# Attention then a squared-ReLU MLP on one core: query tiles 1 and 3 of batch 0 moved from an f32 path to an f16 one, with a new instruction order

## The chip, the cores and the metric

The kernel runs on one core of a Trainium2 chip. The metric is the device time of one execution in microseconds (us), of which the median over several executions is compared. The core has a matrix engine (TensorE, PE in the profile, its weight loads PEld), a vector engine (VectorE, DVE), a scalar engine (ScalarE, ACT), a general engine (GpSimd, POOL), and SyncE (SP), whose queue issues every transfer of this kernel, in order. Each engine works through its own queue in order and waits where an operand is not ready.

## What is computed

The reference, cut to what matters (4 batches, 8 heads, 576 positions, head dimension 64; then 2304 rows of 512 through 2048 hidden values):

```python
q_rot, k_rot = (rotate(q), rotate(k))
scores = scale * np.matmul(q_rot, k_rot.transpose(0, 1, 3, 2))
scores = scores - np.max(scores, axis=-1, keepdims=True)
attn = np.exp(scores)
attn = attn / (np.sum(attn, axis=-1, keepdims=True) + 1e-09)
x = np.matmul(attn, v)            # heads joined to rows of 512
h = x @ w_in
r = np.maximum(h, 0.0)
out = (s * (r * r) + b) @ w_out
```

The result has to hold f32 accuracy.

## The kernel before, in words

**Tiles.** Heads are taken in pairs; a batch has four pairs, the kernel sixteen, numbered 0 to 15. A pair has nine query tiles of 128 rows: 0 to 3 and 4 to 7 are its main rows (two tiles for each head in each half), 8 holds the last 64 rows of both heads. Half a batch's rows form a *unit* of the MLP: tiles 0 to 3 of batch 0 are unit 0, tiles 4 to 7 of batch 0 are unit 1, and so on up to unit 7; unit 8 is all the tiles 8.

**One query tile** (`attend`, line 185) is: scores on PE into PSUM (`s_tile`, lines 590 to 603), their minimum after scaling on DVE (`s_max`, line 609), the exponential and its sum on ACT (`s_exp`, through the helper on line 372), a reciprocal on DVE (line 637). Then the probabilities have to be transposed and multiplied by V, and for that there are two paths.

- **The f16 path** splits every f32 number into two f16 numbers, high and low. `p_a` writes the high part (ACT line 372, DVE line 364 or POOL line 366), `p_b` the low part (DVE line 369), both into the buffer `pab`; `p_t` (line 665) transposes `pab` by a DMA from SP into a `pt` buffer; `pv_sum` (line 687) multiplies with V, in 28 f16 matmuls of 64 weight columns, and ACT (`o_out`) copies the result to `x`. A `pt` buffer has room for two tiles.
- **The f32 path** normalizes in place (`p_norm`), transposes on PE by matmuls with the identity (`p_T`, lines 721 and 723, into the PSUM buffer `po`), copies PSUM to a `pt` buffer (`p_ev`: ACT line 372 or DVE line 711) and multiplies in f32 (`pv32`, line 740).

Which tiles go the f32 path is set by `is_g` on line 116: pairs 0 to 3 (batch 0), tiles below 4 with `i % 2 < GT`. With `GT = 2` those are all of tiles 0 to 3. Both paths' `pt` tiles share two buffers.

**Unit 0** has an MLP of its own in f32 on the unsplit weights (`mlp_in0`, line 833; `mlp_out0`, line 857, with `out_sum0`, which copies `po` to SBUF on ACT). Its two 128-row halves, j = 0 and 1, take the two halves of one `po` buffer. Meanwhile the weights, loaded as f64 bit patterns (`load_w`, line 400) and put together to f32 words (`w_sign`, `w_low`, `w_rebias`, `w_join`, all into the array `wio` through staging buffers `x`), are measured by `w_gram` on PE (line 438) and split into f16 pairs (`w_hi`, `w_lo`, DVE line 369, `wio<-wio,wsc`). Units 1 to 8 run on the f16 pairs: `x_hi` and `x_lo` split the attention output into `xa`, then `mlp_in` (line 807, 12 matmuls for each of 16 blocks f) and `mlp_out` (line 877).

**What sets the order.** `plan()` lists 2690 steps. Three strings fix the rest: `ORDER` is the sequence of the steps (two characters each), `PICKS` the engine of every step that may run on several, `SLOTS` the buffer of every step that takes one. The tables come from a search made ahead of time. In `plan()` several steps that fill different parts of one buffer (the two halves of `po`, for instance) have no edge between them. The framework adds a wait wherever two steps touch one buffer and one of them writes.

```python
GT = 2
def is_g(pr, i):
    return pr < HP and i < 4 and i % 2 < GT
def alone(pr, i):
    return is_g(pr, i) or i == 8 or (GT == 1 and pr < HP and i < 4)
def width(pr, i):
    return 64 if i == 8 else P if GT == 1 and pr < HP and i < 4 else 256
# in attend(), for a tile of the f32 path, and else:
add((ACT, DVE, POOL), "p_norm", *c, r=[("r", (pr, g))], w=[("p", c)])
add(PE, "p_T", *c, r=[("p", c), ("tab",)], w=[("po", c)])
add((ACT, DVE), "p_ev", *c, r=[("po", c)], p=[("pt", pr, "j", t)])
add((ACT, DVE, POOL), "p_a", *c, r=[("p", c), ("r", (pr, g))], p=[("pab", c)])
add(DVE, "p_b", *c, r=[("p", c), ("r", (pr, g))], w=[("pab", c)])
add(DMA, "p_t", *c, r=[("pab", c)], p=[("pt", pr, j // 2)])
```

Of the kernel before, what the change touches and what calls it, by code (L numbers as in the profile page):

```python
# [19 lines left out]
GT = 2  # L20
# [7 lines left out]
B, H, S, D, DM, DFF, P = 4, 8, 576, 64, 512, 2048, 128  # L28
# [9 lines left out]
    "DVAADUDTDoAWDWDXDYDZAQDeDaDlDfDgDbDcDdDpDmDqAZDrAYATASDzARD0AUDsDtD2DnAXD3DhDjAJALAMDiDkADDuD1DvD4DwDxAaAwDyAKAyAFJuAGEC"  # L38
    "AzD5EFJvAbAVJ2EeAEAxD7D6A0AND8JwJxJyENEDEGEQAHEREEAqEHEIEJAcAIAOESJ3EKAjJzAkAdAmAlD_AfAgAeAnEOAPArJ4J5J6ELEPEMEcEdD9EgEh"
    "AtAsEfAoEiAhEqJ0A9A3EVETEWEjEUEkBAA_A4ElA-EZA5J7BBEmAuJ1D-KAKBKIKJEnErBEA6BHAiEoApAvJ8EsA1EzEAFREXEaE2FUEpA2J9KCEvKDEwKE"  # L40
    "J-BFKKKLKFA7EtEuKMBGE5J_EYE0BKEbEBKGKHKNBIA8BME3BRBCKaExKSKOKPBXFBBLFCBUBSKTKbBNBTBVBDBOKUE6KcKVKdK2KQBJBPK3KWE1BYBaBZBb"
# [4 lines left out]
    "McLrMTMRdIMdMUMoMpL9CwE4E7MqMrMzbtbzbyMwC5MeC8MFMSGgFsbubxb0M0MxMyMhb1MfMsC2NOMGM1bvNBbwMiC7C6DGMVNPM2DHM3b2MHDIE8FWb3M7"
    "NCNQE9E-NDDJFXE_FAFHNRMjMgDMM8FYFJC9FZFab4b5CdNmCXM-M4FICeM_MkMlDPNANSNnNTM5FKb9b6b8NpCkCqb_DODNNoGjFNDQNUFqNENFNqCrMtFt"
    "NrFrNsFuNGFLM6FOM9FjFhNJDKNHb-NYNbcAcBcCcJcIb7cHMuNcNZF1NtFkF4NKFiNuNaMvFvFMNINLGEGFFlNxF2F5NvcKNdcLNeNfNycMcUOAcNcTdJcW"
    "NgOBN2N3OCN4NMNNNhF3NiNVFmNjODOEFnOFN5OGdKN6N7cVcXcYFwOOcDcEcFORFxOPFoFyNkNlFzOHF0dLOQdMdNDLC3CxOSC4F7dOdPGIOLOIN8OMFPOT"
# [951 lines left out]
```

## Time and profile before

| what | value |
|---|---|
| median of 3 executions | 642.1 us (642.1, 645.03, 641.84) |
| the profiled execution: its own time | 644.86 us |
| the profiled execution: span, first to last instruction | 643.1 us |
| mean granted TensorE clock, as a share of full speed | 0.970 |
| PE busy | 591.7 us, 92% of the span |
| DVE busy | 478.3 us, 74% |
| ACT busy | 421.8 us, 66% |
| POOL busy | 130.5 us, 20% |
| DMA | 90.67 MB, mean 141 GB/s |

The page of the profile gives each engine's busy time, then the span in 40 slices of 16 us, a digit a slice (9 is 90% or more). PEclk, in the same slices, is the clock that TensorE was granted. Rows of groups, waits and the order of time carry the line of the kernel (L857), the engine, the operation, and the tiles as output<-input. A matmul row's own time is longer than its share of the engine, since matmuls overlap; where it matters, the distance from one start to the next is taken.

### The profile page before, as it was taken

Reading aid. Unit: us, or ns where it says so; the run is one execution under the profiler, and the core shown is the slowest. Engines: PE = TensorE matmul, PEld = TensorE weight load, DVE = VectorE, ACT = ScalarE, POOL = GpSimd, SP = SyncE. Lnnn points to the kernel's source line nnn. Section 1 sums busy time; section 2 is a strip of 40 time slices with the busy share of each in tenths; the row PEclk is TensorE's granted clock in tenths of the full one; section 3 lists DMA queues with packets and bytes.
Section 4 is the critical chain, followed back from the end, with each engine's and each line's share of the span. In section 5 each row is a group of like instructions: output and inputs, shape, how many; then the busy total and the mean of one; then the engine's idle time right before and its main releaser. Section 6 shows DMA issues by size and latency. Waiting matters only on the chain. (4 is left out here: it accounts for less than half of the span.)

```text
span 643.1 us, 13206 instructions
## 1 busy us (share of the span) xinstructions
PE 591.7 (92%) x5054; PEld 398.7 (62%) x5054; DVE 478.3 (74%) x1035; ACT 421.8 (66%) x872; POOL 130.5 (20%) x138
## 2 busy tenths in 40 slices
PE   2356999998979999999989999999999999999996
PEld 2234566677637657667656666667665766766863
DVE  5797989998978999898987898888677355633101
ACT  5686889778878997777667786574673556422411
POOL 0313455211011323121022022102111102110210
PEclk9666999999989999999999999999999999999999
DMA  8899477896937595889546867557465022170100
GB/s 288 248 241 251 159 227 224 211 188 145 184 92 180 120 176 128 193 216 187 112 94 132 168 152 147 130 131 150 107 134 125 20 70 57 32 149 1 34 1 33
DMA packets 207376, 90.67 MB, mean 141 GB/s; under 512 B 189393, under 2 KB 193617, under 8 KB 207313
## 3 DMA queue, kind: packets, MB, share of 16 engines
q1 hardware_dynamic: 207312, 89.83, 59.7%
q8 instruction: 39, 0.64, 0.4%
q14 instruction: 25, 0.20, 0.1%
HBM read 31.97 MB, written 4.72 MB: 57 GB/s over the span
## 5 line engine op out<-in xcount | busy, mean ns | idle before, releaser
L877 PE MATMUL po<-wio,g 128*128 128x512 f16 x768 | 185.2, 379 | 1.0 <-DVE o L369 1.0
L807 PE MATMUL px<-xa,wio 128*128 128x256 f16 x1536 | 183.3, 273 | 0.0
L807 PEld LDWEIGHTS <-wio 128*128 128x128 f16 x1536 | 147.6, 98 | 34.4 <-issue 2.9
L372 ACT ACTIVATE p<-s,nm 128x576 f32<-128x576 f32 x144 | 105.7, 735 | 49.8 <-DVE s L609 35.8
L609 DVE TENSOR_SCALAR_CACHE_REDUCE s<-s,es 128x576 f32<-128x576 f32 x135 | 109.2, 819 | 30.4 <-PE s L603 29.3
L877 PEld LDWEIGHTS <-g 128*128 128x128 f16 x768 | 71.6, 98 | 72.2 <-issue 3.9
L369 DVE SCALAR_TENSOR_TENSOR pab<-p,sum,pab 128x576 f16<-128x576 f32 x128 | 107.0, 846 | 7.9 <-POOL pab L366 3.8
L372 ACT ACTIVATE hr<-px,xc 128x512 f32<-128x512 f32 x64 | 43.7, 683 | 77.5 <-PE px L807 76.3
L825 POOL TENSOR_TENSOR g<-hr,g 128x512 f16<-128x512 f32 x34 | 41.6, 1226 | 225.8 <-DVE g L711 98.7
L372 ACT ACTIVATE pab<-p,sum 128x576 f16<-128x576 f32 x62 | 47.2, 767 | 12.5 <-DVE sum L637 5.6
L366 POOL TENSOR_SCALAR pab<-p,sum 128x576 f16<-128x576 f32 x35 | 31.4, 899 | 118.3 <-DVE sum L637 74.5
L602 PE MATMUL s<-kS,qkT 128*128 128x512 f16 (+1 forms) x150 | 52.6, 386 | 2.1 <-DMA kS<-qkT 2.1
L602 PE MATMUL s<-qkT 128*128 128x512 f16 (+1 forms) x150 | 53.0, 391 | 1.1 <-ACT p L372 1.0
L711 DVE CAST g<-hr 128x512 f16<-128x512 f32 x30 | 12.8, 426 | 54.8 <-ACT hr L372 35.5
L687 PE MATMUL px<-pt,v 128*64 128x256 f16 (+1 forms) x880 | 51.0, 247 | 1.8 <-DMA pt<-pab 1.8
L602 PEld LDWEIGHTS <-qkT 128*128 128x128 f16 (+1 forms) x300 | 28.6, 103 | 32.8 <-issue 8.9
L687 PEld LDWEIGHTS <-v 128*64 128x64 f16 x880 | 36.5, 110 | 14.7 <-issue 12.3
L372 ACT ACTIVATE hr<-hr 128x512 f32<-128x512 f32 x68 | 42.6, 628 | 1.5
L366 POOL TENSOR_SCALAR wio<-x 128x512 bf16<-128x512 f32 (+1 forms) x32 | 28.5, 901 | 58.2 <-ACT x L372 21.1
L833 PEld LDWEIGHTS px<-x,wio 128*128 128x128 f32 x256 | 30.6, 192 | 4.5 <-issue 2.0
L833 PE MATMUL px<-x,wio 128*128 128x128 f32 x256 | 33.0, 280 | 0.1
L603 PEld LDWEIGHTS <-qkT 128*128 128x128 f16 (+1 forms) x300 | 27.8, 101 | 7.6 <-issue 3.2
(137 smaller groups left out, 853.9 us busy)
## 6 DMA issues: line engine op xcount, KB each, us to landing
x<-in_moe_w_in_dram SPq DMA_DIRECT2D x16, 512.0 KB, 5.1
x<-in_moe_w_out_dram SPq DMA_DIRECT2D x16, 512.0 KB, 4.4
st_v<-in_v_dram SPq DMA_DIRECT2D x16, 320.0 KB, 4.0
st_q<-in_q_dram SPq DMA_DIRECT2D x16, 288.0 KB, 3.8
st_k<-in_k_dram SPq DMA_DIRECT2D x16, 288.0 KB, 3.9
kS<-qkT SPq DMA_DIRECT2D x30, 144.0 KB, 2.6
out_dram<-o SPq DMA_DIRECT2D x7, 512.0 KB, 3.4
vS<-v SPq DMA_DIRECT2D x32, 64.0 KB, 2.1
```

The lines of the kernel that those rows point to most:

```text
L366: eng.tensor_scalar(out=out, in0=in0, scalar1=s1, scalar2=s2, op0=op0, op1=op1)
L369: nc.vector.scalar_tensor_tensor(out=out, in0=in0, scalar=scalar, in1=in1, op0=op0, op1=op1)
L372: nc.scalar.activation(out=out, in_=in_, func=func, **kw)
L602: nc.tensor.matmul(ps[rows, MAIN:2 * MAIN], lhs, kk[:, 4 * h:4 * h + 4], start=(n == 0), stop=(n == 1))
L603: nc.tensor.matmul(ps[rows, MAIN - TAIL:MAIN], lhs, kk[:, 8, 64 * h:64 * h + 64], start=(n == 0), stop=(n == 1))
L609: nc.vector.tensor_scalar(out=T["s"], in0=T["s"], scalar1=-1.0 / 8.0 if pr in FQ else st[pr]["es"], scalar2=None, op0=ALU.mult, op1=ALU.mi ...
L687: nc.tensor.matmul(o[64 * h:64 * h + 64, 0:n], v_rows(pr, h, k, z), pv_rhs(pr, i, h, k), start=((z, k) == todo[0]), stop=((z, k) == todo[-1]))
L711: nc.vector.tensor_copy(out, in_)
L807: nc.tensor.matmul(ph, w16[0][:, f, wz, cc], X["xa"][:, xz, c], start=(c == 0 and n == 0), stop=(c == NC - 1 and n == 2))
L825: (nc.vector if eng == DVE else nc.gpsimd).tensor_tensor(out=g[:, 1], in0=r, in1=g[:, 0], op=ALU.subtract)
L833: nc.tensor.matmul(ph, wi[:, f + 1, c * P:(c + 1) * P], xs[0]["x"][:, c, j * P:(j + 1) * P], start=(c == 0), stop=(c == NC - 1))
L877: nc.tensor.matmul(po, g[:, gz, jj], w16[1][:, f, wz], start=(n == 1 and i == 0), stop=(n == NF and i == 2))
```

## The change

`GT` is 1 in place of 2. Of batch 0's query tiles 0 to 3, tiles 1 and 3 (of all four pairs, eight tiles) now go the f16 path, tiles 0 and 2 stay on the f32 path. Unit 0's MLP stays in f32. For the eight tiles `p_norm`, `p_T`, `p_ev` fall away, and `p_a`, `p_b`, `p_t` come in; the four `pv32` of half j = 1 become four `pv_sum` with 128 output columns. All three tables are new: the order of all steps, the picks and the buffers. Nothing else in the file differs (a table is one line shorter, so its lines are numbered one lower).

```diff
-GT = 2
+GT = 1
 ORDER = (
-    "DVAADUDTDoAWDWDXDYDZAQDeDaDlDfDgDbDcDdDpDmDqAZDrAYATASDzARD0AUDsDtD2DnAXD3DhDjAJALAMDiDkADDuD1DvD4DwDxAaAwDyAKAyAFJuAGEC"
...
+    "DTAAEDDUEEECDbDcDdEGDeDhEHEFAQDiEIEQDfDgEREJEKENELAJESEMALATASDjDkJ2DoDqEOEPEVAMEWJ3JuJvAKETADDtAFJ4AEAGAHEUDrDpJ5J6DzAN"
...
 PICKS = (
...
 SLOTS = (
...
```

Four counts from the new order against the old, of what each queue holds ahead of unit 1's first f16 MLP matmul (on PE) and of the `x_lo` or `x_hi` of unit 1 that it needs (DVE, ACT):

| queue | steps before | steps now | what differs |
|---|---|---|---|
| PE | 186 | 175 | `p_T` 16 to 8, `pv32` 8 to 4, `pv_sum` 9 to 12, `mlp_out0` 30 to 28 |
| DVE | 322 | 314 | `p_b` 26 to 32, `p_ev` 4 to 0, `w_lo` 18 to 13, `s_max` 46 to 44, `w_sign` 9 to 12, `w_low` 4 to 6, `p_a` 4 to 2; `p_s` 14 to 10, one `g0`, `p_norm` and `v_hi` less, one `w_hi` more |
| ACT | 240 | 242 | `p_a` 17 to 26, `p_ev` 12 to 8, `p_norm` 11 to 7, `p_s` 18 to 22, `w_hi` 12 to 8, `w_low` 19 to 23, five kinds by one or two |
| SP | transposes among the loads of w_out: 5 before the last load | 8 of tiles 1 and 3 and one more | see the third place below |

**First place: PE, the work on a tile 1 or 3.** Before, in the stretch in which unit 0's tiles are finished (`s` is a score tile, `p` the probabilities, `st_v` V in f32):

```order
L590 MATMUL s_1076<-xa_197,xa_199 128x512
L591 MATMUL s_1076<-xa_197,xa_199 128x64
L721 MATMUL po<-ident,p_1022 128x128 x4
L723 MATMUL po<-ident,p_1022 64x128 x2
L740 MATMUL px_1102<-pt_1008,st_v_270 64x128 x10
L602 LDWEIGHTS qkT_325
```

Now, at the first tile pair of the new path (the two rows of L686 go on in this way to 28 pairs):

```order
L589 MATMUL s_942<-xa_146,xa_181 128x512
L590 MATMUL s_942<-xa_146,xa_181 128x64
L686 LDWEIGHTS v_355
L686 MATMUL px_948<-pt_924,v_355 64x128
L686 LDWEIGHTS v_355
L686 MATMUL px_948<-pt_926,v_355 64x128
```

The transposes are gone from PE, and the product with V reads two `pt` buffers that a DMA fills.

**Second place: ACT, around the copies of unit 0's result** (`o<-po` is `out_sum0`; PE's next `mlp_out0` or `mlp_out` writes `po`). Before, the copy of half 0:

```order
L372 ACTIVATE g_2060<-g_2060,sb 128x512
L372 ACTIVATE wio<-wio,wsc 128x512
L372 ACTIVATE pab_2199<-p_2133,sum_2132 128x576
L372 ACTIVATE o<-po 128x512
L372 ACTIVATE wio<-wio,wsc 128x512
```

and on PE, where this copy falls in between the two rows of `mlp_out0` with x2:

```order
L772 MATMUL px_2149<-g_2130,ones16b 128x256
L857 MATMUL po<-wio,hr_1848 128x512
L382 MATMUL px_2155<-mx,ones_99 128x3
L857 MATMUL po<-wio,hr_1848 128x512 x2
L857 MATMUL po<-wio,g_1951 128x512 x2
L602 LDWEIGHTS qkT_2139
```

Now both copies stand together on ACT:

```order
L371 ACTIVATE pab_2392<-p_2305,sum 128x576
L371 ACTIVATE p_2407,sum_2386<-s_2362,nm_2384 128x576
L371 ACTIVATE o<-po 128x512
L371 ACTIVATE g_2422<-hr_2375 128x512
L371 ACTIVATE o<-po 128x512
```

and PE has all of `mlp_out0` behind it by then; the last rows of it and what follows:

```order
L602 LDWEIGHTS qkT_2175
L602 MATMUL s_2362<-kS_2188,qkT_2175 128x64
L856 MATMUL po<-wio,g_2251 128x512 x4
L381 MATMUL px_2432<-mx,ones_99 128x3
L806 LDWEIGHTS wio
L806 MATMUL px_2434<-xa_2211,wio 128x256
```

The copy of half 0 no longer stands between two matmuls into the same buffer.

**Third place: SP, the loads of w_out** (`x` is a staging buffer of a weight block, `pt<-pab` a transpose). Before:

```order
L400 DMA x_1082<-in_moe_w_out_dram 128x1024
L490 DMA st_v_1164<-in_v_dram 128x640
L400 DMA x_1192<-in_moe_w_out_dram 128x1024
L665 DMA_TRANSPOSE pt_1197<-pab_975 128x9x128
L665 DMA_TRANSPOSE pt_1199<-pab_1115 128x9x128
L490 DMA st_v_1201<-in_v_dram 128x640
```

Now:

```order
L399 DMA x_909<-in_moe_w_out_dram 128x1024
L664 DMA_TRANSPOSE pt_924<-pab_849 128x9x128
L664 DMA_TRANSPOSE pt_926<-pab_671 128x9x128
L399 DMA x_929<-in_moe_w_out_dram 128x1024
L399 DMA x_988<-in_moe_w_out_dram 128x1024
L664 DMA_TRANSPOSE pt_1018<-pab_804 128x9x128
L399 DMA x_1020<-in_moe_w_out_dram 128x1024
```

Eight loads of w_out now stand behind the first of the new transposes, and the last of them (block 12) behind all eight.

## Rows read from the trace of the kernel before

**Rows 1.** The page: busy time of each engine, and TensorE's clock in 40 slices.

```profile
PE 591.7 (92%) x5054; PEld 398.7 (62%) x5054; DVE 478.3 (74%) x1035; ACT 421.8 (66%) x872; POOL 130.5 (20%) x138
...
PEclk9666999999989999999999999999999999999999
```

**Rows 2.** Busy time by stretch (from:to, length, then columns PE, PEld, DVE, ACT, POOL, PEclk, DMA share, GB/s).

```profile
0.00:64.00 64.00, 30.25 (x193) 20.07 (x194) 47.96 (x102) 44.36 (x88) 14.42 (x20) 0.74 0.89 256
64.00:192.00 128.00, 119.26 (x1053) 82.70 (x1052) 116.59 (x274) 108.15 (x232) 38.31 (x45) 0.98 0.73 180
192.00:643.00 451.00, 442.15 (x3811) 295.95 (x3809) 313.76 (x661) 269.33 (x553) 77.75 (x73) 1.00 0.52 114
```

**Rows 3.** PE's waits, 64 to 210 us: total, times, longest.

```profile
PE po L857 <- ACT o L372: 3.6, 1, 3.6
```

**Rows 4.** DVE's waits, 64 to 210 us: total, times, longest.

```profile
DVE s L609 <- PE s L603: 5.9, 5, 3.6
```

**Rows 5.** PE in order of time (start, duration): a `p_T`, what follows it, a `pv32`.

```profile
76.64 0.66 PE L721 MATMUL po<-ident,p 128*128 128x128 f32 x4 [0.21 <-ACT p L372]
...
77.60 0.39 PE L602 MATMUL s<-qkT 128*128 128x512 f16 x1
...
81.22 1.46 PE L740 MATMUL px<-pt,st_v 128*64 128x128 f32 x20 [0.20 <-DVE wmx L441]
```

**Rows 6.** PE in order of time: a `pv_sum` of 64 columns, one of 256, what follows.

```profile
151.89 0.35 PE L687 MATMUL px<-pt,v 128*64 128x64 f16 x10
...
152.45 1.12 PE L857 MATMUL po<-wio,g 128*128 128x512 f32 x2
...
158.14 0.74 PE L687 MATMUL px<-pt,v 128*64 128x256 f16 x10
...
159.79 1.16 PE L833 MATMUL px<-x,wio 128*128 128x128 f32 x8
```

**Rows 7.** PE in order of time: `mlp_out0` ahead of and behind a wait; first f16 `mlp_in`.

```profile
166.52 1.88 PE L857 MATMUL po<-wio,g 128*128 128x512 f32 x4
...
182.76 2.50 PE L857 MATMUL po<-wio,hr 128*128 128x512 f32 x4 [3.62 <-ACT o L372]
185.06 3.10 PE L857 MATMUL po<-wio,g 128*128 128x512 f32 x4
...
193.85 2.78 PE L807 MATMUL px<-xa,wio 128*128 128x256 f16 x24
```

**Rows 8.** PE by stretch of 4 us (columns PE, PEclk, DMA share, GB/s).

```profile
180.00:184.00 4.00, 1.24 (x3) 1.00 0.69 164
184.00:188.00 4.00, 4.00 (x7) 0.57 0.00 0
```

**Rows 9.** ACT in order of time: the copy that PE waited for.

```profile
182.13 0.58 ACT L372 ACTIVATE o<-po 128x512 f32<-128x512 f32 x1
```

**Rows 10.** Groups of instructions by shape on DVE (count, busy us, mean ns).

```profile
L609 DVE TENSOR_SCALAR_CACHE_REDUCE s<-s,es 128x576 f32<-128x576 f32 x135 | 109.2, 819 | 30.4 <-PE s L603 29.3 <-ACT p L372 0.9
L369 DVE SCALAR_TENSOR_TENSOR pab<-p,sum,pab 128x576 f16<-128x576 f32 x128 | 107.0, 846 | 7.9 <-POOL pab L366 3.8 <-ACT pab L372 3.8
...
L369 DVE SCALAR_TENSOR_TENSOR wio<-wio,wsc 128x512 f16<-128x512 f32 x32 | 24.0, 750 | 1.0 <-POOL wio L366 0.5 <-ACT wio L372 0.4
...
L364 DVE TENSOR_SCALAR pab<-p,sum 128x576 f16<-128x576 f32 x31 | 16.5, 538 | 0.5
...
L364 DVE TENSOR_SCALAR wio<-x 128x512 uint16<-128x512 uint16 x13 | 7.3, 560 | 4.9 <-ACT x L372 3.5 <-DMA x<-in_moe_w_in_dram 0.6 <-DMA x<-in_moe_w_out_dram 0.5
...
L711 DVE COPY pt<-po 128x640 f32<-128x640 f32 x4 | 3.3, 821 | 0.0
```

**Rows 11.** The transposes of line 665: duration on SP (ns, min/median/max), then issue to landing.

```profile
L665 SPq DMA_TRANSPOSE pt<-pab x128: 1242/1308/2727, 103.7 to 575.8; - x128
...
DMA to landing us min/median/max: 2.8/2.9/5.6
```

**Rows 12.** DVE in order of time: its first rotation.

```profile
7.06 0.76 DVE L527 TENSOR_TENSOR z<-st_q,tab 128x576 f32<-128x576 f32 x1 [1.52 <-DMA st_q<-in_q_dram]
```

More of the change, by code (lines that the diff above doesn't have):

```diff
@@ new lines @@
+    "KtBaBZBYDnBbBKFQBLLUKeJ_KqK-BxABKrKuBMKvKfBNKYLaKQA1K_BOByLABzB0LbKwLBB1KRLVLWKZBeBJBgFFKxBhBfBPBQA2LcK2KgKhBwLIBWBcKyB2"
+    "BkBnB4B7BiLdLeLJBdK3FsB-FSBmLKK4KzCBLLB6BlB5BoB8BjBpLiL0BqLCFGB_CAB3L1LMLDK5LfCSK6LjCCCTLgLEK0FUCUK1KiKjCVboLNCWL2LkLOFD"
+    "dBCLE4COE7CDB9MICNL3CMClbpL-bmbnCEMJL4CPLlCYFTL5CnMKL_CmCoCpLPLXCZCyFVK7CbbqL6CaEbCcMLMMLmLYLZE8K8FbbrMAbsCsMmdCC1C0CvLn"
+    "CuMBE9MndDLodECtLhCFCGCwdFMCE-CzE_MNMoMpdGFAGGMDFvMqC2MEFedHbtbubvMZb0byLpCfMOCIdIMPFfCHLqLsMaLtLrCiCgChCJCjFHFILuMQLvbw"
@@ new lines @@
+    "CXbzbxCdMWFcCeLwMXC_K9LFb1MTb2FJLGLxMULyLHMYDMDGDOMbMcDBDIb8b-CKCQMwMzMRFgFdCRDAMdDCMxM0L7LzFqMeMfDDb_L8MrMyL9M1DJb9NOFt"
+    "MsNPMFC5NBNQMGNmMHFKC6MhM2DHMiNncTdJb3cAcBNCcVcWcUMVMSGFC8NRNSNoM-CqCkMjMgb4dKDKM3NTNUDPCrM_GIM7cXNDcYC7M4GSM5M8F1MkNpFW"
+    "dLcZMlDNNANENqNrcCb5FXdMFYb6DENYb7C9FZFaNFNZFNNGNsC3CxC-C4DFFLMtNJcacbDQMuDRdNGJFjFkDLNbcccDcENKNHM6M9FOMvFhNcNdNaNLNIFi"
+    "NtFPODdOcFOANuNeNxNfOEDSNgFrGENjFlF2OBNvdnNhF3NkNMNVdPdQOCNyNwNzFMOFFnOGOHNNcKcHcIOON2NWcJGHN3FuNXN4OIOPN5cLOLcMcNcgORce"
@@ new lines @@
+    "NlNiGgFoFwcfcdchOSdROTGPGQGROJOQFxF4N6dSFyFzOUOMOVN7ciOZOsOecGcjOfGTckOgF0OaOtN0OvcsclcqGBOwF5N8OWOuN1dTF6dUOxdVF9docrcp"
+    "cOOhcmOXdpGUdqF-drdWctcuOyFmOKN9GCONGfOiOzF7dXdYN-OjN_O3cvO8O0OkdZdscPGKO9GDO4O-ObOYOlOmdaGLF8FpdbGjOpGMGNGOOnOqdccncoPN"
+    "cwO_PAOcOdeRc3cxeScyddcQGbPBPCGiPKHUGeG6G9F_O5eTdeO1eUGAO2POdfeVeWPDeXPLPEeYeZPPPMPQeadgPRGsebGVGXGYHXPSc0c2czQWc1cRdhc4"
+    "c5PVdiPaPbQXPTdjdkedecOrOoc6PHeeefdlQYenemO6Pdc7PFPIGtGhdmQZeodtepGWGpduQaPePcO7egQbPGG4GZG5PUc8c9c-PfGqdvehdwGaPJGcc_eq"
@@ L89 @@
[L89 to L91 removed]
+    "GSSVVSGSSVSSGVSGVSGSGVSSVSSGSSGSSVSGVVGGSSGVSGSSGSSVSGGGSGGSVSSGSSVSSGVGGSSGSGGSSVGGGSSVSGVSGGSGVVSSSVVSSSVVSSSVVGSSVVSS"
+    "SVVSGSVVSSGGVGGSVVSSSVVGSSVVSGSGVSGVVVSSSVVSSSVGSGGVVGSSSSSSSSSSSSVSVSSSSSSSSVSSSSVSSGVSVSSSSGSSSSSSSSSVSSVGSSSSVSVSSSSS"
@@ L104 @@
+    "210100101102000011020130213110304211113002011110010022340011030110210101101342120131100310111303002101231100041120121311"
+    "132011030101010114030001101120110102130110130211004102011112000001030301101210101101323010010201000410501043010100001021"
+    "100002362201410131001101132100043201000100102114011210301410000103110002001110110041103110100121130021011021010011401111"
+    "00010110120021010010100013301011142032010104001003011043110210004110110200231101000110012101010010020010"
 )
```

99 lines of the change are left out of this document (40 added, 59 removed).

## The prediction

> **What bounds the kernel now.** I read the page first. Over the whole span PE is busy 92% of the time [rows 1], so whatever shortens PE's queue is worth looking at; but an average says nothing of the stage that the change touches. So the next view is busy time by stretch [rows 2], and it shows three stages. In 0 to 64 us PE does 30.25 us of work and the granted clock is 0.74: PE is waiting for loads and for the work on DVE and ACT. In 64 to 192 us, where batch 0 is finished and unit 0 has its f32 MLP, PE is busy 119.26 of 128 us (93%), but DVE is busy 116.59 (91%) and ACT 108.15 (84%). From 192 us on PE has 442.15 us of work in 451 us, and DVE only 313.76. The first f16 MLP matmul, that of unit 1, starts at 193.85 us [rows 7]. It is my milestone: behind it PE alone paces the kernel, so the change gains what it brings that matmul forward, less what work it leaves over for later.
>
> The waits say what the idle time of the middle stage is. The largest single one on PE is 3.62 us, for a copy on ACT [rows 3]: the first `mlp_out0` of half 1 writes the other half of the `po` that `out_sum0` of half 0 reads, and starts at 182.76 [rows 7], right after the copy of 0.58 us that began at 182.13 [rows 9]. What the wait leaves behind is seen in two more rows. PE was busy only 1.24 of the 4 us before 184, and the granted clock of the next 4 us is 0.57 [rows 8], so near the lower of its two levels (1.2 GHz, half of 2.4). The two L857 rows there take 2.50 and 3.10 us, where the same row at full clock took 1.88 [rows 7]. DVE waits for a score tile for up to 3.6 us [rows 4]: PE's queue holds that tile behind the stalled matmul.
>
> **The change part by part.** *PE, work.* A `p_T` took from 76.64 to 77.60, 0.96 us [rows 5]; eight fall away, 7.7 us. A `pv32` took 1.46 [rows 5]; four fall away, 5.8 us. Four `pv_sum` of 128 columns come in. The trace has none of that width, so it is bounded by the two next to it: with 64 columns 151.89 to 152.45, 0.56 us, with 256 columns 158.14 to 159.79, 1.65 us [rows 6]. By the line between them 128 columns take 0.56 + 1.09/3 = 0.92, and four 3.7 us (bounds 2.2 and 6.6). PE's work: -7.7 - 5.8 + 3.7 = **-9.8 us**.
>
> *PE, the stall.* In the new order (second place) both `out_sum0` stand behind all of `mlp_out0`, and between the last `mlp_out0` and the next write to `po` PE has unit 1's first `mlp_in`, each more than 1 us of work (2.78 for the row of two [rows 7]) against two copies of 0.58 us. So the 3.6 us go, and with them the slow clock's extra (2.50 + 3.10 - 2 x 1.88 = 1.84). If the cover were gone, a wait of the same size would be back. If PE alone set the pace, the sum would be -9.8 - 3.6 - 1.8 = **-15.2 us**.
>
> *DVE.* But DVE is as full as PE in this stage, and the `x_lo` of unit 1, which the first f16 `mlp_in` reads, is on its queue. I priced the difference of the two queues ahead of `x_lo` (the table of counts) with the mean durations [rows 10]: six more `p_b` at 0.846, +5.1; four `p_ev` less at 0.821, -3.3; five `w_lo` less at 0.750, -3.8; two `s_max` less at 0.819, -1.6; three `w_sign` and two `w_low` more at 0.560, +2.8; two `p_a` less at 0.538, -1.1; and for the handful of others (four small `p_s`, a `g0`, a `p_norm` and a `v_hi` less, a `w_hi` more) an estimate of -2 between 0 and -3. Together -3.9. DVE also loses the 3.6 us in which it waited behind the stalled PE [rows 4], since the score tile now stands ahead of the last `mlp_out0` rows. The new order loads k before q; DVE's first rotation waited 1.52 us for q [rows 12], so I take up to 1.5 of that, the other bound being zero. So DVE lets the milestone come -3.9 - 3.6 - 1.5 = 9.0 us earlier. What it comes ahead of must still be done: two `mlp_out0` steps (half a four-matmul row each, 0.94, together 1.9 [rows 7]) and one wide `pv_sum` (1.65 [rows 6]) are moved behind it, +3.5. Paced by DVE the change gives **-5.5 us**.
>
> *ACT, POOL, DMA.* ACT has 242 steps in place of 240 ahead of its `x_hi`, nine `p_a` more against four `p_ev`, four `p_norm` and four `w_hi` less, and it was busy 84%: level, priced at zero. The cover is its 20 us of slack in these 128; with it gone, two steps of some 0.6 us would cost 1 us. POOL takes over some of the rotations; it is busy 38.31 of 128 us [rows 2], so nothing is added there, and what it does late would be seen only behind the milestone. The eight new transposes each hold SP 1.31 us and land 2.9 us after issue [rows 11]; with a DMA share of 0.73 in the stage [rows 2] I price them at zero if SP has the loads of w_out out in time (its rival is below).
>
> *Behind 192 us* PE's work is the same but for the 3.5 us above. PE idles 8.9 of 451 us there [rows 2]; the new order could make that more or less by a few us, at most all 8.9 on the side of gain, and I take zero.
>
> **The sum.** The two bounds are -5.5 (DVE paces) and -15.2 (PE paces). DVE's share of the stage is two points below PE's, so some of PE's gain does come through, but the milestone hangs on DVE's queue: I take -7.5, nearer that end. The sum is made against the profiled execution, 644.86 us (a span of 643.1 and 1.76 outside it). The median of the runs is 642.1, that is 2.8 lower; I carry the difference over to the median, **634.5 us**. A measurement of this kernel can tell about 0.5% from no change, 3.2 us: faster is below 638.9, slower above 645.3.
>
> **Rivals.** *A, the forecast:* a gain of 4 to 11 us, 631 to 638 us. For it: both engines lose work, and the removed wait is a real one, with DVE's wait hanging on it. Chance 0.50.
>
> *B, PE paces all of it:* DVE was filled with splitting weights and can do that later, so PE's 15.2 us come through whole, 627. For it: five `w_lo` have already left DVE's queue. Against it: PE's queue needs `x_lo` in order. Chance 0.15.
>
> *C, the gain is handed back:* PE's saved work turns into idle time, because in the new order PE arrives earlier at score tiles, `pt` buffers or halves of `po` that DVE, ACT and SP don't have ready. One new wait of the removed one's size, with the slow clock behind it, is 3.6 + 1.8 = 5.4 us, which takes -5.5 to about zero: 642, and with it 639 to 645. The case that the change doesn't do what its words say of `po` is in here too: two copies of 0.58 us would have to end before `mlp_out` writes, and if ACT does them late, the wait is back at another place. For it: DVE and ACT are at 91% and 84%, so a new order has little slack to hide a late step in. Chance 0.21.
>
> *D, slower:* in the new order eight transposes stand among the loads of w_out on SP (third place), the last block's load behind all of them. SP issues in order, and a transpose waits there for its `p_b`; each holds it 1.31 us, so that load leaves 8 x 1.31 = 10.5 us later, and so do the pieces `w_sign`, `w_low`, `w_join` and the `w_gram` of the block, at which PE, in order, stands. This gives -5.5 + 10.5 + 1.8 (the clock after a stall) = +6.8, 649. It decides from the point at which the delay exceeds the 5.5 us of gain; below that the loads' lead hides it. For it: DVE is the late engine, and `p_b` is its work. Against it: the transposes of before stand among those loads as well (five ahead of the last). Chance 0.14.
>
> The Trainium skill, page "VectorE: DVE Perf Modes", speaks against the change as well: its section "Rules for kernel authors" gives 128x128 transposes to TensorE where PSUM will do as the destination, and its section "The three transpose paths" prices the DMA crossbar at 1309 ns a block against TensorE's 390. By that figure nine blocks would take 11.8 us (an estimate from that page), and the eight tiles 94 us of transfer. The trace does not agree: nine blocks land 2.9 us after issue [rows 11], so the measurement decides, and the rule has no share in rival D's price or chance.
>
> **How the numbers follow.** Faster is A and B, 0.65; same is C, 0.21; slower is D, 0.14. The range runs from B's 627 to C's upper end 645: it leaves out D and the part of B below 627, hardly 2 in 10. The bounds of the small unknowns (`pv_sum` 2.2 to 6.6, the start 0 to 1.5, the others on DVE 0 to -3) move the forecast by 3 us at most and lie within it.
>
> **What the profile would show.** If the steps are right: PE's wait of L856 for ACT's copy is gone, the granted clock stays near 1.0 in the middle stage, the first f16 `mlp_in` (L806 now) starts near 185 in place of 193.85, DVE's wait of 3.6 us for a score tile is gone, and PE's busy time over the span falls by some 10 to 12 us to about 580. If B holds, it starts near 179. If C, PE's busy time falls just as much, but PE's idle time grows by the same, in one or two rows of its waits. If D, w_gram on PE (L437) waits for several us on pieces of the last w_out blocks. The forecast is wrong in its reasoning, whatever the time, if the milestone comes no earlier and the gain arises behind it, or if the opening stage before 64 us moves by more than 2 us.

## The result, and the profile after

The changed kernel takes 638.06 us (median of 6, 636.74 to 639.68) against 642.8 us of the one before (median of 6, 641.84 to 645.48): a ratio of 0.9919, 95% interval 0.9893 to 0.9945. Timed once more beside other kernels it took 638.42 us against 644.4, ratio 0.9916 (0.9887 to 0.9944). So it is faster by 5 to 6 us, 0.8%. The forecast was 634.5 with a range of 627 to 645: the sign and the range held, the size was forecast about half as large again as it is.

The page of the changed kernel: busy time of each engine.

```profile
PE 586.2 (92%) x5022; PEld 392.3 (62%) x5022; DVE 476.7 (75%) x1027; ACT 426.9 (67%) x888; POOL 126.3 (20%) x130
```

Its busy time by stretch (from:to, length, PE, PEld, DVE, ACT, POOL, PEclk, DMA share, GB/s).

```profile
0.00:64.00 64.00, 34.92 (x238) 21.79 (x238) 54.61 (x124) 51.17 (x104) 11.27 (x18) 0.92 0.93 282
64.00:192.00 128.00, 116.39 (x1038) 80.33 (x1038) 118.48 (x258) 108.45 (x235) 33.51 (x38) 0.96 0.83 191
192.00:635.70 443.70, 434.91 (x3750) 290.15 (x3748) 303.63 (x647) 267.32 (x552) 81.49 (x75) 1.00 0.55 114
```

Beside [rows 2]: behind 192 us nothing has changed but the amount of work, PE idles 8.8 us there as before. The new thing is the opening, in which VectorE does 54.61 us of work in place of 47.96. The granted clock of the opening, 0.92 against 0.74, is not what the change brings: the profiled executions of e2 and e12 below, which keep the old opening, show 0.93 and 0.68 there, at equal medians. And in the middle stage PE idles 11.6 us (128 - 116.39), where it idled 8.7 although the kernel before still had the stall on `po` in there. PE's waits in that stage:

```profile
PE px L686 <- DMA pt<-pab: 5.5, 6, 1.4
PE px L437 <- DVE wio L368: 3.4, 1, 3.4
```

The wait of [rows 3] is gone. In its place `pv_sum` waits six times for a transpose, 5.5 us in all, and `w_gram` once for VectorE, 3.4 us. Then PE in order of time: the cost of a `pv_sum` of 128 columns, a slow row behind such waits, the first f16 `mlp_in`, and what is left of unit 0 behind it.

```profile
90.46 4.75 PE L856 MATMUL po<-wio,hr 128*128 128x512 f32 x6
...
98.34 0.47 PE L686 MATMUL px<-pt,v 128*64 128x128 f16 x10
...
99.25 0.39 PE L601 MATMUL s<-qkT 128*128 128x512 f16 x1
...
182.36 5.41 PE L806 MATMUL px<-xa,wio 128*128 128x256 f16 x48
...
189.85 3.68 PE L856 MATMUL po<-wio,g 128*128 128x512 f32 x8
```

A 128-column `pv_sum` takes 99.25 - 98.34 = 0.91 us. At 90.46, right behind four short waits (0.44, 0.69, 0.47 and 0.65 us between 84.9 and 88.9 us), six `mlp_out0` matmuls take 4.75 us where 2.82 would be due (1.88 for four, [rows 7]); the granted clock from 88 to 92 us is 0.50, the lower of its two levels. So the slow clock came along with the new waits too. The first `mlp_in` starts at 182.36 against 193.85 [rows 7], 11.5 us sooner; four `mlp_out0` steps (3.68 us) are still to be done behind it, two more than before. The milestone splits each kernel into two parts. Here they are for before (first two rows) and for the changed kernel, each in its own fence:

```profile
0.00:193.85 193.85, 151.36 (x1248) 103.44 (x1249) 166.40 (x378) 154.17 (x322) 52.73 (x65) 0.90 0.78 205
193.85:643.10 449.25, 440.30 (x3807) 295.28 (x3805) 311.91 (x658) 267.67 (x551) 77.75 (x73) 1.00 0.52 113
```

```profile
0.00:182.36 182.36, 141.67 (x1188) 94.76 (x1189) 163.45 (x365) 150.05 (x317) 43.47 (x54) 0.94 0.89 229
182.36:635.70 453.34, 444.55 (x3836) 297.51 (x3834) 313.27 (x663) 276.90 (x572) 82.80 (x76) 1.00 0.54 113
```

Ahead of the milestone PE has 9.7 us less work and only 1.8 us less idle time (42.5 to 40.7); behind it lie 4.2 us more work, and the stretch is 4.1 us longer. Together -7.4 us between the two profiled executions (643.1 to 635.7 us of span; their own times are 644.86 and 637.53). That is more than the medians differ, because the profiled execution of before was 2.1 us above its median in this set and that of the changed kernel 0.5 below. (In the later sets the median of before, over 11 to 23 executions, is 644.3 to 644.6.)

### The profile page after: what moved, and what is told of

Read it like the earlier page. It is cut to its first block, busy times and chain, and to the rows that moved or that the text cites. A ratio compares the mean times of both kernels' runs of the same rounds, so it can differ in the third digit from the quotient of the medians.

```text
span 635.7 us, 13159 instructions
## 1 busy us (share of the span) xinstructions
PE 586.2 (92%) x5022; PEld 392.3 (62%) x5022; DVE 476.7 (75%) x1027; ACT 426.9 (67%) x888; POOL 126.3 (20%) x130
## 4 chain that ended last, share of the span: by engine, by line
PE 76%; DMA 7%; DVE 6%; issue 5%; ACT 4%; POOL 1%; SPq 1%; DVEq 0%; ACTq 0%; POOLq 0%
PE po L876 24%; PE px L806 24%; PE px L686 8%; PE s L601 8%; DMA pt<-pab 4%; PE po L856 4%; PE px L832 2%; ACT p L371 2%; DVE wio L368 1%; PE s L602 1%; DVE s L608 1%; PE s L589 1%; DMA st_k<-in_k_dram 1%; DVE pab L368 1%; DMA x<-in_moe_w_in_dram 1%
## 5 line engine op out<-in xcount | busy, mean ns | idle before, releaser
L368 DVE SCALAR_TENSOR_TENSOR pab<-p,sum,pab 128x576 f16<-128x576 f32 x136 | 115.7, 859 | 10.1 <-ACT pab L371 8.8
L824 POOL TENSOR_TENSOR g<-hr,g 128x512 f16<-128x512 f32 x30 | 37.4, 1246 | 213.1 <-ACT g L371 90.0
L686 PE MATMUL px<-pt,v 128*64 128x256 f16 (+2 forms) x960 | 56.0, 245 | 8.3 <-DMA pt<-pab 8.3
L371 ACT ACTIVATE pab<-p,sum 128x576 f16<-128x576 f32 x73 | 55.0, 766 | 6.3 <-issue 2.0
L686 PEld LDWEIGHTS <-v 128*64 128x64 f16 x960 | 39.8, 110 | 24.5 <-issue 15.5
L365 POOL TENSOR_SCALAR pab<-p,sum 128x576 f16<-128x576 f32 x32 | 29.5, 926 | 119.4 <-DVE sum L636 72.6
L371 ACT ACTIVATE hr<-hr 128x512 f32<-128x512 f32 x68 | 42.5, 627 | 1.5
L710 DVE CAST g<-hr 128x512 f16<-128x512 f32 x22 | 9.7, 439 | 35.1 <-ACT hr L371 33.2
L365 POOL TENSOR_SCALAR wio<-x 128x512 bf16<-128x512 f32 (+1 forms) x23 | 20.1, 884 | 54.3 <-ACT x L371 23.0
```

What stands on the lines that cost most here:

```text
L365: eng.tensor_scalar(out=out, in0=in0, scalar1=s1, scalar2=s2, op0=op0, op1=op1)
L368: nc.vector.scalar_tensor_tensor(out=out, in0=in0, scalar=scalar, in1=in1, op0=op0, op1=op1)
L371: nc.scalar.activation(out=out, in_=in_, func=func, **kw)
L686: nc.tensor.matmul(o[64 * h:64 * h + 64, 0:n], v_rows(pr, h, k, z), pv_rhs(pr, i, h, k), start=((z, k) == todo[0]), stop=((z, k) == todo[-1]))
L824: (nc.vector if eng == DVE else nc.gpsimd).tensor_tensor(out=g[:, 1], in0=r, in1=g[:, 0], op=ALU.subtract)
```

## The experiments

Two theories went into the first set. **Q:** VectorE's queue paces the stage, and the gain comes from the new order (a denser opening, the removed stall). **P:** the 9.8 us of work that PE loses carry it. Edits to the order are shown as steps, in the sequence in which the order lists them; most steps that stay in place are left out.

**e1: the path alone.** The old order, with each new step in the place of the one that it replaces, for tiles 1 and 3 of pairs 0 to 3 (here pair 0):

```diff
-GT = 2
+GT = 1
-p_norm (0,1)
+p_a (0,1)
+p_b (0,1)
...
-p_T (0,3)
-p_ev (0,3)
-p_T (0,1)
-p_ev (0,1)
+p_t (0,1)
+p_t (0,3)
...
-pv32 (0,1)
+pv_sum (0,3)
```

> The kernel before with its own order, picks and buffers; only the path is changed: tiles 1 and 3 of batch 0 go the f16 path, each new step in the place of the one it replaces (p_a and p_b for p_norm, both p_t where p_T of tile 3 stood, pv_sum for pv32). Theory Q (VectorE's queue paces the stage; the gain of the change comes from the new order, that is a denser opening and the removed po stall): -3 to +3 us against before, PE busy about 5 to 10 us less, the 3.6 us wait for out_sum0 still there. Theory P (the 9.8 us of work that PE loses carry the gain): -5 to -9 us, with nothing left for the order to bring.

Measured: 663.89 us against 644.49, ratio 1.0304 (1.0259 to 1.0348): 19 us slower. Neither theory had that. The order of the `s_max` on VectorE is the same in both kernels, so the same instruction can be laid beside itself. In before, then in e1 (VectorE in order of time):

```profile
70.11 0.75 DVE L609 TENSOR_SCALAR_CACHE_REDUCE s<-s 128x576 f32<-128x576 f32 x1
...
109.96 0.81 DVE L609 TENSOR_SCALAR_CACHE_REDUCE s<-s,es 128x576 f32<-128x576 f32 x1
...
228.52 0.81 DVE L609 TENSOR_SCALAR_CACHE_REDUCE s<-s,es 128x576 f32<-128x576 f32 x1
```

```profile
67.78 0.75 DVE L608 TENSOR_SCALAR_CACHE_REDUCE s<-s 128x576 f32<-128x576 f32 x1
...
126.24 0.83 DVE L608 TENSOR_SCALAR_CACHE_REDUCE s<-s,es 128x576 f32<-128x576 f32 x1 [3.17 <-PE s L602]
...
244.67 0.81 DVE L608 TENSOR_SCALAR_CACHE_REDUCE s<-s,es 128x576 f32<-128x576 f32 x1
```

e1 is 2.3 us ahead at 70, 16.3 behind at 110, and 16.2 behind at 228: 18.6 us are lost in the 40 us in which the eight tiles are finished, and only some 2 more by the end (the two profiled spans are 18.2 us apart). How long SP's queue waits at transposes for `p_b` between 60 and 130 us, in before and in e1:

```profile
SPq L665 <- DVE pab L369: 2.8, 2, 2.1
```

```profile
SPq L664 <- DVE pab L368: 12.1, 4, 4.8
```

SP stands at transposes (L664) for `p_b`, and the loads of w_out stand behind them: the last of the 16 leaves at 133.2 us in e1 and at 116.9 in before. That is the picture of rival D, and about a third of the loss can be followed through it. SP, GpSimd, VectorE and PE of e1 in order of time:

```profile
70.73 8.11 SPq L664 DMA_TRANSPOSE pt<-pab  x2
78.93 0.53 SPq L399 DMA_DIRECT2D x<-in_moe_w_out_dram  x1
...
83.04 0.76 POOL L365 TENSOR_SCALAR wio<-x 128x512 uint16<-128x512 uint16 x1 [8.33 <-DMA x<-in_moe_w_out_dram]
...
84.55 0.46 DVE L363 TENSOR_SCALAR wio<-x 128x512 uint16<-128x512 uint16 x1 [1.56 <-POOL x L365]
...
89.33 0.74 PE L686 MATMUL px<-pt,v 128*64 128x128 f16 x10 [6.63 <-DVE xw L363]
```

Two transposes hold SP for 8.1 us, and the load behind them leaves at 78.93. GpSimd stands 8.3 us for a load of w_out, VectorE 1.6 us for GpSimd and soon after 2.0 for ACT, which had stood 1.9 for another load of w_out. The first `pv_sum` then stands 6.6 us on PE, although its own transposes had landed at 74.3 and 80.4 us: it is released, as the trace has it, by a copy out of PSUM (`xw`) on VectorE, which comes at 89.12 us, against 83.26 in before. The two kernels were level at 75 us, so 5.9 us are lost on this way. The rest of the 18.6 has not been followed; e6, e8 and e9 below look at the same rival. The slow clock may have a part in the loss: the mean granted clock is 0.75 between 60 and 135 us in e1, and 0.96 in before between 60 and 118.7, which is about the same work.

**e2: one step moved.** Order, picks and path of before, but `out_sum0` of half 0 late:

```diff
 mlp_out0 (1,5)
-out_sum0 (0)
 x_hi (1)
 mlp_out0 (1,6)
...
 mlp_out0 (1,15)
+out_sum0 (0)
 out_sum0 (1)
```

> The kernel before with one step moved: out_sum0 of half 0 stands right in front of out_sum0 of half 1, behind all of mlp_out0. Theory Q: the wait of 3.6 us and the slow clock behind it go, x_lo comes up to 3.6 us sooner, -3 to -5 us against before. Theory P, and the rival that the wait only moves on: 0 to -1 us, with another wait of 2 us or more on PE between 180 and 200 us.

Measured: 638.17 us, ratio 0.9898 (0.9861 to 0.9934), a little more than theory Q's 3 to 5 us. **One step moved is worth as much as the whole change.** Three `s_max` of before, and below them the same three of e2:

```profile
184.18 0.82 DVE L609 TENSOR_SCALAR_CACHE_REDUCE s<-s,es 128x576 f32<-128x576 f32 x1
...
188.69 0.82 DVE L609 TENSOR_SCALAR_CACHE_REDUCE s<-s,es 128x576 f32<-128x576 f32 x1 [3.64 <-PE s L603]
...
208.18 0.82 DVE L609 TENSOR_SCALAR_CACHE_REDUCE s<-s,es 128x576 f32<-128x576 f32 x1
```

```profile
186.02 0.82 DVE L609 TENSOR_SCALAR_CACHE_REDUCE s<-s,es 128x576 f32<-128x576 f32 x1
...
186.75 0.82 DVE L609 TENSOR_SCALAR_CACHE_REDUCE s<-s,es 128x576 f32<-128x576 f32 x1
...
204.63 0.82 DVE L609 TENSOR_SCALAR_CACHE_REDUCE s<-s,es 128x576 f32<-128x576 f32 x1
```

Ahead of the stall e2 happened to run 1.84 us behind; past it, it is 3.55 us ahead. The stall is worth 5.4 us, which is what the prediction's two terms for it make (3.6 and 1.8). VectorE's queue takes none of it back, since it had been waiting for the score tile behind the stalled matmul. What e2 doesn't show is that the changed kernel gains by the same thing: its order differs everywhere, and what the rest of it gains and loses can't be separated from the stall.

**e3 and e4: the openings exchanged.**

```diff
-new order, steps 1 to 2690
+old order (with the new path), steps 1 to 300, then the others in the new order
```

```diff
-old order, steps 1 to 2690
+new order, steps 1 to 262 (none of the f16 path), then the others in the old order
```

> The changed kernel with the opening of the one before: the first 300 steps in the old order (q before k, the old turn of loads and weight blocks), the rest in the new. Theory Q: VectorE's idle time before 64 us goes back from 9.4 to about 16, and the time is 4 to 7 us above the changed kernel's, so within 2 us of before. Theory P: the opening does not matter, within 2 us of the changed kernel.

> The kernel before with the opening of the changed one: the first 262 steps of the new order (these hold no step of the f16 path), the rest in the old order, the path as before. Theory Q: VectorE idles some 3 to 6 us less before 64 us, and the time is 2 to 6 us below before. Theory P: within 1.5 us of before.

Measured: e3 704.44 us, ratio 1.0916 (1.0864 to 1.0968); e4 736.21, ratio 1.1409 (1.1362 to 1.1456). These two say little about the opening. Its part did move: VectorE is busy 47.94 us in the first 64 in e3 (54.61 in the changed kernel), 52.77 in e4 (47.96 before). But e3, which has the opening of before, ends 60 us above before, and e4 ends 92 us above it: that is lost behind the seam, the step at which the second order takes over. Presumably the progress of loads, weight blocks and tiles that the rest of that order counts on is not there; this was not followed in the traces. How much the denser opening is worth by itself stays open.

**e5: the changed kernel again; e6 and e7: cover for `pv_sum`.** e6 moves four `pv_sum`, each with its `o_out`, some steps later; e7 also mends the 3.4 us wait of `w_gram`:

```diff
-pv_sum (1,3)
 all_sum (4)
 s_tile (1,8)
+pv_sum (1,3)
...
-pv_sum (0,8)
 mlp_in0 (1,1)
+pv_sum (0,8)
...
-pv_sum (0,7)
 mlp_out0 (0,7)
+pv_sum (0,7)
...
-pv_sum (1,8)
 mlp_out0 (0,9)
+pv_sum (1,8)
```

```diff
-w_low (1,2)
 w_sign (0,15)
+w_low (1,2)
...
-w_join (1,2)
 rotate (4,q)
+w_join (1,2)
```

> The changed kernel once more, beside the three others of this set. Both theories: 0.988 to 0.995 of before, as at first. If its ratio lies within 0.4% of that of the kernel in which only the copy was moved (0.990), the path and the rest of the new order together bring nothing over that one step.

> The changed kernel with four pv_sum (and their o_out) moved a few steps later on TensorE, so that other matmuls stand between them and the transposes that they read: (1,3) behind the s_tile of (1,8), (0,8) behind the mlp_in0 of (1,1), (0,7) behind the mlp_out0 of (0,7), (1,8) behind the mlp_out0 of (0,9). Theory W (the path gives its 9.8 us of saved PE work back as waits for transposes, 5.5 us with a slow clock behind some of them): 3 to 6 us below the changed kernel. Theory Q (VectorE's queue paces the stage, PE's waits there are slack): within 2 us of it, while PE's waits for pt fall from 5.5 to under 2 us.

> As the kernel before it in this set, and on GpSimd w_sign of block (0,15) goes ahead of w_low of block (1,2), which waits for a load; w_join of (1,2) goes behind the rotation of q of pair 4 on VectorE. In the changed kernel VectorE waited 1.9 us there and TensorE 3.4 us (w_gram). Theory Q: VectorE comes 1 to 2 us sooner to x_lo, and the time is 1 to 2 us lower than that of the kernel before it in this set. Theory W: 2 to 4 us lower, by PE's wait.

Measured: e5 638.42 us, ratio 0.9916 (0.9887 to 0.9944), within 0.2% of e2's 0.9898. So over what e2 gives, the path and the rest of the order together bring nothing that can be measured; the two intervals leave room for some 3 us either way. e6 646.25 us, 1.0038 (1.0015 to 1.006); e7 646.58, 1.0022 (0.9994 to 1.0049). Both theories are wrong here: PE's waits for transposes did fall (5.5 to 3.2 us in e6), its waits for probabilities from ACT rose (1.7 to 8.3 us between 60 and 192 us), and the kernel is 8 us slower. SP's queue in the changed kernel, and the same issues in e6 (`SPq` is the queue, in order of time):

```profile
87.19 1.30 SPq L664 DMA_TRANSPOSE pt<-pab  x1
88.60 0.53 SPq L399 DMA_DIRECT2D x<-in_moe_w_out_dram  x1
```

```profile
90.15 1.30 SPq L664 DMA_TRANSPOSE pt<-pab  x1
91.55 0.52 SPq L399 DMA_DIRECT2D x<-in_moe_w_out_dram  x1
```

The later `pv_sum` gives its `pt` buffer back later, the next transpose waits for it on SP, and the load of w_out behind it leaves 3 us late (91.55 against 88.60). VectorE then stands for just such a block, in e6:

```profile
DVE wio L363 <- DMA x<-in_moe_w_out_dram: 3.6, 1, 3.6
```

At 90 us the two kernels are level (0.1 us), at 98 e6 is 3.7 us behind; a second step, of 4.6 us between 130 and 140 us, has the transposes behind `pv_sum` of (0,7), which SP issues at 133.15 in place of 126.32. A `pv_sum` that waits for its transpose is thus no waste here: it sits at the earliest place, and that is what turns the two `pt` buffers round.

**e8: more room in the old order.** As e1, with each of its four `pv_sum` some 20 steps later and the next pair's transposes behind it:

```diff
-pv_sum (0,3)
 s_tile (0,5)
...
 w_gram (1,2)
+pv_sum (0,3)
+p_t (1,1)
+p_t (1,3)
```

> The kernel of the first set with only the path changed (+19 us), with more room in the order: each of its four pv_sum stands some 20 steps later, and the transposes of the next pair behind it. If that kernel lost its time because TensorE stood in order at each pv_sum for transposes that were just issued: 6 to 14 us lower than it. If it lost it because the transposes on SP's queue hold back the loads of w_out behind them (rival D): still within 4 us of it, with SP standing at transposes for 10 us or more between 60 and 130 us.

Measured: 672.15 us, ratio 1.0415 (1.0379 to 1.0452), 8 us above e1. PE no longer stands at `pv_sum`, but SP stands longer at transposes for PE (12.0 us in two waits, the longest 9.8, between 60 and 130 us). More room at `pv_sum` makes it worse. So e1 doesn't lose its time by PE standing at `pv_sum` alone; since the next transposes, and the loads behind them, moved later too, the run doesn't say more.

**e9 to e11: loads of w_out off SP's queue.** In e1, in the changed kernel, and in e6:

```diff
-        nc.sync.dma_start(out=t.rearrange("p m t -> p (m t)"), in_=(w_in, w_out)[which][f].bitcast(U32))
+        (nc.gpsimd if which else nc.sync).dma_start(out=t.rearrange("p m t -> p (m t)"), in_=(w_in, w_out)[which][f].bitcast(U32))
```

> The kernel with only the path changed (664 us), and the 16 loads of w_out issued by GpSimd in place of SyncE, at the same places of the order. Theory D (the transposes on SP's queue, waiting there for p_b and for a free pt buffer, hold back the loads behind them, and VectorE and TensorE stand for the weight blocks): 6 to 14 us below it, 650 to 658. If the loss comes from the transposes themselves (their landing, the two pt buffers) and not from what stands behind them: within 4 us of 664. A bound against both: GpSimd stands in order at a load whose staging buffer is not free, and its own p_a and w_sign come late; then slower than 664.

> The changed kernel with the 16 loads of w_out issued by GpSimd in place of SyncE. Theory D: the new order has already put the loads where the transposes do little to them, so 0 to 3 us below the changed kernel, and PE's waits for pt (5.5 us) fall, since the transposes no longer wait behind loads. If GpSimd standing at loads delays its own work: 2 to 8 us above.

> The changed kernel with four pv_sum moved later (646 us, 8 above the changed kernel), and the 16 loads of w_out issued by GpSimd. There a first step of 3.6 us came where VectorE waited for a load of w_out that stood on SP behind a transpose waiting for the pt buffer of the late pv_sum; a second of 4.6 us at 130 to 140 us, behind the last loads. Theory D: the first step goes, the second stays: 642 to 644. If the loads were not the cause: 645 to 648.

Measured: 676.97 us (ratio 1.0494, 1.0457 to 1.0532), 661.82 (1.028, 1.0233 to 1.0327) and 663.06 (1.0311, 1.027 to 1.0352). All three are slower. The bound named ahead of e9 was that GpSimd now issues and converts in one queue. GpSimd's waits between 60 and 150 us, in e9 (first two rows) and in e1:

```profile
POOL wio L365 <- DMA x<-in_moe_w_out_dram: 23.8, 8, 4.1
POOL x L399 <- DVE sum L636: 6.3, 2, 4.0
```

```profile
POOL wio L365 <- DMA x<-in_moe_w_out_dram: 30.2, 7, 8.3
```

It stands for landing loads in both, less in e9 than in e1. New in e9 is the wait at the issue of a load itself (L399), 6.3 us in two places, as the bound had it; whether that makes up the 13 us by which e9 is slower than e1 isn't shown. So e9 and e10 don't decide for or against rival D. The pair e10 and e11 says something: with the loads off SP, the four late `pv_sum` cost 1.2 us (within the intervals); with the loads on SP they cost 8. That fits the loads behind the transposes as the way in which e6 lost its time. It is not proof, since the move off SP cost 23 us and 17 us by itself first.

**e12: a second wait removed from e2.** On ScalarE, two steps change places:

```diff
-p_a (3,8)
 mlp_in0 (1,2)
 mlp_r0 (1,0)
 mlp_r0 (1,0)
+p_a (3,8)
```

> The kernel before with two steps moved and the path as before: out_sum0 of half 0 late, as in the second run, and on ScalarE the two mlp_r0 of (1,0) ahead of p_a of (3,8). In the second run ScalarE stood 3.6 us at that p_a, with mlp_r0 behind it, and TensorE 2.06 us for mlp_r0's PSUM buffer (w_gram at 147 us), the next mlp_out0 row at half clock (1.96 in place of 1.02). If such waits of TensorE in this stage are worth their length and the slow rows behind them: 2 to 3 us below the second run, 635 to 636.5, which would be below the changed kernel too. If VectorE's queue has slack to take it back: within 1 us of the second run (638.2).

Measured: 638.17 us, ratio 0.9895 (0.987 to 0.9921): the same as e2 in the median. The trace shows the wait gone. PE in before, in e2, then in e12:

```profile
146.95 0.62 PE L438 MATMUL px<-wio 128*128 128x128 bf16 x8 [1.95 <-ACT hr L372]
147.41 1.07 PE L857 MATMUL po<-wio,g 128*128 128x512 f32 x2
```

```profile
147.12 0.62 PE L438 MATMUL px<-wio 128*128 128x128 bf16 x8 [2.06 <-ACT hr L372]
147.57 1.96 PE L857 MATMUL po<-wio,g 128*128 128x512 f32 x2
...
190.21 2.78 PE L807 MATMUL px<-xa,wio 128*128 128x256 f16 x24
```

```profile
144.74 0.85 PE L438 MATMUL px<-wio 128*128 128x128 bf16 x12
145.43 1.07 PE L857 MATMUL po<-wio,g 128*128 128x512 f32 x2
...
187.60 2.78 PE L807 MATMUL px<-xa,wio 128*128 128x256 f16 x24
```

The slow row behind the wait doesn't always come: in before the same wait, 1.95 us long, left the next row at 1.07 us, in e2 it takes 1.96, at a granted clock of 0.50 from 148 to 150 us. The first `mlp_in` comes 2.6 us sooner than in e2, and the span of the profiled execution is 1.7 us shorter (639.0 to 637.3), but the medians are equal, and the executions of each kernel spread over 2 to 4 us. A gain of this size can't be told here. No version ran that is clearly below the changed kernel.

## Why the prediction was right, and where it was not

**The stall on `po`: right, with its price.** 3.6 and 1.8 us were forecast for the wait and the slow rows; e2 shows 5.4 us between two rows of the same order, and 6.3 us (4.3 to 9.0 by the interval) in the median.

**That DVE paces the milestone: right in sum, wrong in its parts, and not shown.** The sum said that `x_lo` of unit 1 comes 9.0 us sooner; it started at 190.10 and now starts at 180.91, 9.2 us. In before, then in the changed kernel (VectorE's `x_lo`, and busy time up to it):

```profile
190.10 1.28 DVE L369 SCALAR_TENSOR_TENSOR xa<-x,xs,xa 128x1024 f16<-128x1024 f32 x1
...
0.00:190.10 190.10, 147.61 (x1226) 101.41 (x1228) 162.65 (x374) 150.76 (x315) 52.73 (x65) 0.90 0.79 207
```

```profile
180.91 1.27 DVE L368 SCALAR_TENSOR_TENSOR xa<-x,xs,xa 128x1024 f16<-128x1024 f32 x1
...
0.00:180.91 180.91, 140.22 (x1182) 94.12 (x1183) 162.00 (x364) 148.60 (x314) 43.47 (x54) 0.94 0.89 229
```

VectorE's work fell by 0.65 us, not by the 3.9 of the step "DVE". Its idle time fell by 8.5 (27.4 to 18.9), not by 3.6 + 1.5. Most of that is in the opening, 6.65 us (from 16.04 to 9.39 idle in the first 64 us, [rows 2] and the row above), where the prediction had "up to 1.5" and wrote that its reasoning would be wrong if the opening moved by more than 2 us. In that it was wrong: two errors of opposite sign made a right sum, which is luck. In the middle stage, where the 3.6 us were to come from, VectorE's idle time ahead of `x_lo` fell only from 11.4 to 9.5 us.

Nor does PE stand for `x_lo` in either kernel. In before `x_lo` ends at 191.38 us and PE's rows run on without a gap to the first `mlp_in` at 193.85; now it ends at 182.18, and PE comes to `mlp_in` at 182.36, again without a gap. So of the 11.5 us by which the milestone moved, 9.2 are the way of `x_lo` and 2.3 are PE's own; with the 4.1 us of work left over this makes the -7.4 between the two profiled executions. The -2 that the prediction added to -5.5 for "some of PE's gain" has about that size, though no row was given for it.

**What failed: the step "DVE", with "POOL ... nothing is added there".** The work term was put at -3.9 us and measured -0.65. The rows that fit the gap are those that VectorE shares in time with GpSimd. VectorE and GpSimd in the changed kernel, in order of time:

```profile
142.57 0.81 DVE L368 SCALAR_TENSOR_TENSOR pab<-p,sum,pab 128x576 f16<-128x576 f32 x1
143.30 1.90 DVE L368 SCALAR_TENSOR_TENSOR wio<-wio,wsc 128x512 f16<-128x512 f32 x1
145.12 1.95 DVE L368 SCALAR_TENSOR_TENSOR pab<-p,sum,pab 128x576 f16<-128x576 f32 x1
```

```profile
142.74 1.92 POOL L526 TENSOR_TENSOR z<-st_k,tab 128x576 f32<-128x576 f32 x1 [4.13 <-DVE st_k L530]
144.83 1.63 POOL L528 TENSOR_TENSOR st_k<-st_k,tab 128x576 f32<-128x576 f32 x1 [0.17 <-ACT junk L371]
```

A `w_lo` that takes 0.75 us takes 1.90, a `p_b` of 0.81 takes 1.95, while a rotation runs on GpSimd; the same two rows take 1.90 and 1.95 in e5, a second execution of this kernel. Among single `p_b` and `w_lo` rows before 200 us, the 7 that overlap a GpSimd row take 1.29 us on average and the 40 others 0.78, so the overlap costs 7 x 0.51 = 3.5 us, about the 3.25 between forecast and measurement. In before only 3 rows overlapped, at 0.79. This is an agreement of sums, not a trial: no run moved these rotations away. It isn't that GpSimd has more to do: it has three rotation steps ahead of the milestone in either kernel, and 43.47 us of work there in place of 52.73. The prediction looked at how busy GpSimd is and not at what runs on VectorE at the same time.

**PE's work: its prices right, its total not settled, its gain not to be seen.** A 128-column `pv_sum` was put at 0.92 us and takes 0.91. Ahead of the milestone PE has 9.7 us less to do, but 4.2 of them have only moved behind it: over the span PE's busy time fell by 5.5 us, to 586.2, where the prediction's signs had 10 to 12 and about 580. One execution of each kernel can't say how much of that is the change, since e2 and e12, with the f32 path of before, are busy 596.3 and 593.5 us against its 591.7. The sign that the granted clock stays near 1.0 in the middle stage held only nearly (0.96, and 0.98 before). Against e2, which has its milestone at 190.21 us with 155.95 us of work and 34.3 idle ahead of it, the changed kernel has 14.3 us less work there, 6.4 us more idle time and 4.2 us more work behind: 3.3 us between those two executions, nothing between the medians. (Of the 14.3, 4.6 are the difference between e2 and before, which do the same 1248 matmuls there.) Where it went: 5.5 us of waits for transposes and 3.4 for `w_gram`, which the prediction had in rival C, "the gain is handed back", at 0.21.

**Work left over.** +3.5 forecast, 4.1 measured.

**Rival D: a real mechanism, avoided here.** In the old order the path costs 19 us, lost in the 40 us in which transposes stand on SP among the loads; in the new order they are placed so that it doesn't show. There the last load of w_out leaves at 114.0 us, ahead of the 116.9 of before. That the loss passes through the loads rests on the rows of e1 between 70 and 89 us, on e6's row of VectorE and on SP's waits; the direct trial (e9) didn't decide it. The price differs from the prediction's: what holds the loads is SP's wait for `p_b` (12.1 us), more than the 1.31 us that each transpose takes.

**The step to the median.** -7.5 was taken against a profiled execution that ran 2.1 us above its kernel's median, and -7.4 is what the two profiled executions differ by. The medians differ by 4.7 to 6.0. So the gain that the prediction took from rows of single executions was 1.5 to 2.8 us too large for the medians; between two single executions some 2 us are chance. The forecast of 634.5 was low by that, and because it was carried over to a median of three executions (642.1) that was itself low: the later medians of before are 642.8 and 644.3 to 644.6.

## What to carry to other kernels

Look first for the one wait that is written by the order itself, here a copy between two matmuls into halves of one buffer: moving that step gave the whole 0.8% that a new path with a new order gave. Taking work off an engine that is busy 93% of a stage brought nothing that could be measured here, where the new steps wait in an in-order queue that also feeds the others; price a moved step by everything that stands behind it there, and by the buffer that it holds. And when a measured sum agrees, compare its parts as well.

## What was not expected of the hardware

Two engines that don't wait for each other's queues slow each other: `w_lo` and `p_b` on VectorE more than double (0.75 to 1.90, 0.81 to 1.95 us) beside a rotation on GpSimd. The Trainium skill, page "SBUF — State Buffer", section "SBUF: two separate sides", says that a VectorE instruction with two SBUF inputs and a GpSimd instruction that reads SBUF need the same port pair, which the one that starts first holds for its whole instruction while the other blocks. The rows agree with it, and the prediction should have drawn on it: the `p_b` that started at 142.57, ahead of the rotation, kept its 0.81 us, and the rotation took 1.92 (1.41 for a step of the same kind in before).

A slow stretch of TensorE's clock can follow even short waits: six matmuls take 4.75 us for 2.82 behind waits of 0.4 to 0.7 us, and two take 1.96 for 1.07 behind one of 2.06. It doesn't follow each of them: behind 1.95 us in before the two took 1.07.
